# Attention scores in pairs of pairs, a split first eviction and a held value load, in a talking-heads and two-FFN kernel

## The chip, the cores and the metric

The kernel runs on one core of a Trainium2 chip. The metric is the device time of one execution in microseconds (us), lower is better. PE is the matrix engine, PEld its weight loads, DVE the vector engine, ACT the scalar engine, POOL and SP the two engines that here only issue DMAs.

## The reference

Two batches, 12 heads, 448 positions, head size 64, all in float32.

```
scores = einsum('bhij,hg->bgij', q @ k.T / 8, w_pre)      # mix over heads
attn   = softmax(scores)                                   # minus max, exp, over sum
attn   = einsum('bhij,hg->bgij', attn, w_post)             # mix over heads again
x      = (attn @ v)  as (896 tokens, 768)
x      = (h * sigmoid(1.702 h)) @ w_out,  h = x @ w_in     # 768 -> 2048 -> 768
x      = (P(h) / Q(h)) @ w_out2,          h = x @ w_in2    # rational activation
```

## The kernel before, in words

**Attention.** Each batch's 448 query rows are cut into chunks of 120, 120, 120 and 88: eight chunks. For one chunk, `scores` (L293) makes the raw scores of six **pairs** of heads. The two heads of a pair have 64 rows of contraction each, so their two matmuls stand in the two halves of the PE array and run side by side; one pair fills one of two PSUM buffers `mm` (two banks, one head in each). `scores_out` (L295, copies at L229 on ACT and L231 on DVE) evicts a pair to the SBUF tile `S`. When all six pairs of a chunk are in `S`, SP issues its `regroup` DMAs (L313), one for each **group** of 10 query rows: they lay 10 rows by 12 heads on 120 partitions (`T`). A group then goes through `pre` (L318, the first head mix on PE), `rowmax` on DVE (L324), `expo` on ACT (L330), three small steps on DVE or ACT (L336 to L344) that put 1/sum into the second mixing matrix `W`, `post` (L351, the second head mix, four matmuls) and `post_out` (L229, to `AT`). There are 90 groups. After a chunk's last group, `av` (L370) multiplies by `v`, 24 matmuls for each half of the heads.

**The two FFNs.** They begin in the last groups' shadow (L576 to L578 up, L643 to L645 down). Their weights are loaded by POOL's queue and worked on by ACT and DVE during attention and after it.

**Order.** Nothing is ordered by a run-time scheduler. `Plan.issue` (L103) lays out all steps ahead of time: each step has an engine (or several to choose from), an assumed length, the steps it depends on, the buffers that it takes and gives back, and a rank; a free engine gets the ready step of lowest rank whose buffers are free. The result is one fixed order for each engine; on the chip, semaphores make an instruction wait for its inputs. Where PE would be idle for long in the plan, `fill` (L221, L223) puts in matmuls on a tile of ones (`warm`).

**Start.** SP issues six loads of `k` (one for each pair, L280), then the mixing matrices, then the second chunk's `q`; ACT issues the first chunk's `q`; POOL issues the four loads of the first batch's `v` (L285), with nothing to wait for on the chip. The first chunk's pairs are evicted by ACT or DVE, one engine a pair, as the plan chooses (`sco0`).

Of the kernel before, what the change touches and what calls it, by code (L numbers as in the profile page):

```python
# [20 lines left out]
CP = 112  # L21
NJ = S // CP
NP = H // 2
# [43 lines left out]
class Plan:  # L67
# [9 lines left out]
        self.fill = fill  # L77
        self.fill_from = fill_from

    def add(self, name, ways, deps, rank, emit=None, take=(), give=(), lag=0):  # L80

        assert name not in self.steps
        self.steps[name] = (list(ways), list(deps), rank, emit, take, give, lag)

    def taker(self, n, b):

# [16 lines left out]
    def issue(self):  # L103
        steps, slots = self.steps, self.slots
        succ = {n: [] for n in steps}
        left, at, on = {}, dict.fromkeys(steps, 0), {}
        for n, s in steps.items():
            left[n] = len(s[1])
            for d in s[1]:
                succ[d].append(n)  # L110
        idle = dict.fromkeys(("sp", "pe", "act", "dve", "pool"), 0)
        ready = {e: [] for e in idle}
        dry = set()
        events = [(0, 1, n) for n in steps if not left[n]]
        heapq.heapify(events)
        order = []

        runs, more = [], sum(s[0][:1] != [] and s[0][0][0] == "pe" for s in steps.values())

        def busy(now):  # L120
            return sum(min(z, now) - max(a, now - FILL_WIN) for a, z in runs if z > now - FILL_WIN)

        def done(n, now):
            for b in steps[n][5]:
                b, h = b if isinstance(b, tuple) else (b, self.taker(n, b))
                slots[b][slots[b].index(h)] = None
                dry.clear()
            for m in succ[n]:
                who = [w[0] for w in steps[m][0]]
                hop = HOP.get((on.get(n), who == [on.get(n)]), 0) + 80 * (who == ["pe"]) if who else 0  # L130
                at[m] = max(at[m], now + hop)
                left[m] -= 1
                if not left[m]:
                    heapq.heappush(events, (at[m], 1, m))

        while events and events[0][0] < 1e8:
            now = events[0][0]
            while events and events[0][0] == now:
                _, kind, n = heapq.heappop(events)
                if kind == 0 or (kind == 1 and not steps[n][0]):  # L140
                    done(n, now)
                elif kind == 1:
                    for e, ns, wait in steps[n][0]:
                        if wait:
                            heapq.heappush(events, (now + wait, 3, (n, e, ns)))
                        else:
                            insort(ready[e], (steps[n][2], n, ns))
                            dry.discard(e)
                elif kind == 3 and n[0] not in on:
                    insort(ready[n[1]], (steps[n[0]][2], n[0], n[2]))  # L150
                    dry.discard(n[1])
            for e in idle:
                if idle[e] > now:
                    continue
                for _, n, ns in () if e in dry else ready[e]:
                    take, lag = steps[n][4], steps[n][6]
                    if n not in on and all(self.pick(b) is not None for b in take):
                        for b in take:
                            k = self.bank[n, b] = self.pick(b)
                            slots[b][k] = n  # L160
                            self.uses[b] = k + 1
                        ready[e] = [x for x in ready[e] if x[1] not in on and x[1] != n]
                        idle[e] = now + ns
                        on[n] = e
                        heapq.heappush(events, (now + ns + lag, 0, n))
                        heapq.heappush(events, (now + ns, 2, n))
                        order.append(n)
                        if e == "pe":
# [34 lines left out]
def talking_heads_then_two_ffn(ctx: ExitStack, tc: tile.TileContext, q, k, v, wpre, wpost, win1, wout1, win2, wout2, ab, out):  # L203
# [73 lines left out]
    def load_k(b, hp):  # L277
        if hp == 0:
            t_["k", b] = ap1.tile([128, NP, S], F32, tag="k", name=f"k{b}")
        sp.dma_start(t_["k", b][:, hp], k[b, :, hp])  # L280

    def load_v(b, jc):
        if jc == 0:
            t_["v", b] = ap1.tile([CP, NJ, H * D], F32, tag="v", name=f"v{b}")
        (sp if b else pool).dma_start(t_["v", b][:, jc], v[b, :, jc])  # L285

# [5 lines left out]
            r = slice(o * 64, o * 64 + 64)  # L292
            pe.matmul(p[:M, o, :S], t_["q", ci][r, hp, :M], t_["k", b][r, hp], start=True, stop=True)  # L293

    def scores_out(ci, hp, eng):  # L295
        M = CHUNKS[chunks[ci][1]][1]
        if hp == 0:
            if two_s(ci):

                if ci < NC:  # L300
                    x = f(keep.tile([128, 2, KK, S], F32R, tag="x1", name=f"S{ci}")).rearrange("p a k s -> p (a k) s")
                else:
                    x = f(keep.tile([128, H * S], F32R, tag="wu", name=f"S{ci}")).rearrange("p (h s) -> p h s", h=H)
                t_["S", ci] = x[:IC]
            else:
                t_["S", ci] = ap1.tile([IC, H, S], F32, tag="S", name=f"S{ci}")
        cast(eng, t_["S", ci][:M, 2 * hp : 2 * hp + 2], t_["sc", ci, hp][:M, :, :S])

    def regroup(t):
        ci, gi, n, _ = groups[t]  # L310
# [113 lines left out]
        plan.add(name, (), deps, 0, give=give)  # L424

    step(("mixld",), "sp", 900, [], RANK["k"] + 0.5, load_mix, lag=DMA_LAG)
    step(("mix",), "dve", 200, [("mixld",)], -2, scale_mix)
    for b in range(B):
        f0 = first[b * NC]
        for hp in range(NP):  # L430
            step(("kld", b, hp), "sp", 640 if b else 800, [("scdone", b * NC - 1)] if b else [], f0 + RANK["k"] + 0.01 * hp, load_k, b, hp, take=[] if hp else ["k"], lag=DMA_LAG)
        for jc in range(NJ):
            d0 = [("av", b * NC - 1, 1)] if b else [("rg", 5)]
            step(("vld", b, jc), "sp" if b else "pool", 640, d0, f0 + RANK["v"] + RANK["step_v"] * jc, load_v, b, jc, take=[] if jc else ["v"], lag=DMA_LAG)
    for ci, (b, c) in enumerate(chunks):
        M = CHUNKS[c][1]
        f0, l0 = first[ci], last[ci]
# [1 line left out]
        d0 = [("kld", 0, NP - 1)] if ci == 1 else [("qld", ci - 1)] if ci else []  # L439
        step(("qld", ci), "sp" if ci else "act", 683, d0, f0 + RANK["q"] - 20 * (ci == 1), load_q, ci, take=["q"], lag=DMA_LAG)  # L440
        for hp in range(NP):
            step(("sc", ci, hp), "pe", 800, [("qld", ci), ("kld", b, hp)], f0 + RANK["sc"] + 0.1 * hp, scores, ci, hp, take=["mm"])
            d0 = [("sco", ci, 0)] if hp else []
            step(("sco", ci, hp), copying(2 * S, "sco" if ci > 1 else "sco0", True), 0, [("sc", ci, hp)] + d0, f0 + RANK["sco"] + 0.1 * hp, scores_out, ci, hp, None, take=[] if hp else ["S2" if two_s(ci) else "S"], give=["mm"])
        mark(("scdone", ci), [("sc", ci, hp) for hp in range(NP)], [("q", ("qld", ci))] + ([("k", ("kld", b, 0))] if end_b else []))
        for t in range(f0, l0 + 1):
            step(("rg", t), "sp", 1200, [("sco", ci, hp) for hp in range(NP)], t + RANK["rg"], regroup, t, take=["T"], lag=RG_LAG if ci else 2500)
# [10 lines left out]
        mark(("rgdone", ci), [("rg", t) for t in range(f0, l0 + 1)], [("S2" if two_s(ci) else "S", ("sco", ci, 0))])  # L458
        for a in range(2):
            d0 = [("av", ci, 0)] if a else [("phi", t) for t in range(f0, l0 + 1)] + [("vld", b, jc) for jc in range(NJ)]  # L460
            fin = [("AT", ("phi", f0))] + ([("v", ("vld", b, 0))] if end_b else []) if a else []
# [405 lines left out]
```

## Time and profile before

| what | value |
|---|---|
| runs shown | 728.86, 726.19, 727.99 us; median 727.99 us |
| profiled execution, own time | 726.84 us |
| its span, first to last instruction | 725.1 us |
| PE busy | 712.6 us (98% of the span) |
| DVE / ACT / POOL busy | 559.4 / 408.2 / 159.2 us |

The profiled execution's time is 1.74 us more than its span, which lies before the first and after the last instruction, and 1.15 us under the median. The rows come from that execution; times in them count from the start of the span. Matmuls overlap in the rows (one starts before the one ahead has ended), so what PE spends on a piece of work is read from the start of one row to the start of the next.

### The profile page before, as it was taken

Reading aid. Unit: us, or ns where it says so; the run is one execution under the profiler, and the core shown is the slowest. Engines: PE = TensorE matmul, PEld = TensorE weight load, DVE = VectorE, ACT = ScalarE, POOL = GpSimd, SP = SyncE. Lnnn points to the kernel's source line nnn. Section 1 sums busy time; section 2 is a strip of 40 time slices with the busy share of each in tenths; the row PEclk is TensorE's granted clock in tenths of the full one; section 3 lists DMA queues with packets and bytes.
Section 4 is the critical chain, followed back from the end, with each engine's and each line's share of the span. In section 5 each row is a group of like instructions: output and inputs, shape, how many; then the busy total and the mean of one; then the engine's idle time right before and its main releaser. Section 6 shows DMA issues by size and latency. Waiting matters only on the chain.

```text
span 725.1 us, 11626 instructions
## 1 busy us (share of the span) xinstructions
PE 712.6 (98%) x4224; PEld 599.7 (83%) x4224; DVE 559.4 (77%) x1108; ACT 408.2 (56%) x762; POOL 159.2 (22%) x296
## 2 busy tenths in 40 slices
PE   7999999999999999999999999999999999999997
PEld 4567657666677889999999999999999999999996
DVE  0577877677988579888988888978999589879732
ACT  3686676776677455455443444338887565356310
POOL 1023422222322243433432333210001101000000
PEclk9999999999999999999999999999999999999999
DMA  6667877497646364555545454322102211200122
GB/s 199 228 187 257 255 277 254 150 281 250 231 135 206 122 221 145 200 167 181 192 144 185 153 174 153 133 80 73 44 24 72 88 37 58 66 30 19 39 80 103
DMA packets 39368, 106.86 MB, mean 147 GB/s; under 512 B 6478, under 2 KB 19022, under 8 KB 39310
## 3 DMA queue, kind: packets, MB, share of 16 engines
q0 software_dynamic: 22848, 76.89, 32.4%
q1 hardware_dynamic: 16318, 28.85, 12.0%
q8 instruction: 33, 0.54, 0.3%
q10 hardware_dynamic: 144, 0.37, 0.1%
q14 instruction: 25, 0.20, 0.1%
HBM read 71.49 MB, written 15.34 MB: 120 GB/s over the span
## 4 chain that ended last, share of the span: by engine, by line
PE 66%; DMA 2%; DVE 1%; ACT 1%; issue 0%; ACTq 0%; DVEq 0%; SPq 0%
PE mm L643 11%; PE mm L645 11%; PE mm L644 11%; PE bk L577 11%; PE bk L578 11%; PE bk L576 10%; DMA d1d<-wmk 1%; PE bk L351 1%; DMA d1u<-wm 1%; PE bk L370 1%; PE bk L318 0%; DMA cab<-in_ab_dram 0%; ACT L586 0%; DVE wu L234 0%; ACT wmk L535 0%
## 5 line engine op out<-in xcount | busy, mean ns | idle before, releaser
L643 PE MATMUL mm<-g,wd 128*128 128x448 f32 x384 | 141.9, 370 | 0.0
L645 PE MATMUL mm<-g,wd 128*128 128x448 f32 x384 | 140.5, 366 | 0.0
L644 PE MATMUL mm<-g,wd 128*128 128x448 f32 x384 | 140.4, 366 | 0.0
L351 PEld LDWEIGHTS bk<-W,E 120*112 120x112 f32 (+1 forms) x720 | 84.1, 177 | 36.6 <-issue 22.7
L351 PE MATMUL bk<-W,E 120*112 120x120 f32 (+1 forms) x720 | 89.2, 269 | 1.0 <-ACT E L330 0.8
L318 PE MATMUL bk<-T,wpr 120*120 120x448 f32 (+1 forms) x180 | 82.8, 552 | 1.0 <-DVE xh L234 0.5
L530 POOL DMA_DIRECT2D rawk<-in_win_dram x81 | 44.3, 554 | 163.5 <-ACT rawk L523 34.5
L643 PEld LDWEIGHTS mm<-g,wd 128*128 128x128 f32 x384 | 72.2, 188 | 5.8
L645 PEld LDWEIGHTS mm<-g,wd 128*128 128x128 f32 x384 | 72.2, 188 | 5.7
L644 PEld LDWEIGHTS mm<-g,wd 128*128 128x128 f32 x384 | 72.3, 188 | 5.3
L324 DVE TENSOR_REDUCE sm<-bk 120x1 f32<-120x448 f32 (+1 forms) x90 | 55.8, 620 | 26.2 <-PE bk L318 25.7
L576 PE MATMUL bk<-xh,wu 128*128 128x448 f32 x192 | 70.7, 368 | 1.5 <-ACT t L586 1.5
L577 PE MATMUL bk<-xh,wu 128*128 128x448 f32 x192 | 70.3, 366 | 0.5 <-DVE wu L234 0.5
L577 PE MATMUL bk<-xn,wu 128*128 128x448 f32 x192 | 70.4, 367 | 0.0
L576 PE MATMUL bk<-xn,wu 128*128 128x448 f32 x192 | 70.4, 367 | 0.0
L578 PE MATMUL bk<-xn,wu 128*128 128x448 f32 x192 | 70.4, 367 | 0.0
L578 PE MATMUL bk<-xh,wu 128*128 128x448 f32 x192 | 70.2, 366 | 0.0
L237 DVE TENSOR_TENSOR yt<-mm,yt 128x896 f32<-128x896 f32 (+1 forms) x43 | 40.2, 936 | 37.0 <-PE mm L645 36.8
L229 ACT ACTIVATE AT<-bk 112x480 f32<-112x480 f32 (+1 forms) x87 | 50.4, 579 | 30.7 <-PE bk L351 30.0
L530 POOL DMA_DIRECT2D rawk<-in_wout_dram x70 | 38.5, 555 | 103.2 <-ACT W L342 18.7
L330 ACT ACTIVATE E<-bk,sm 120x448 f32<-120x448 f32 (+1 forms) x90 | 56.3, 627 | 2.6 <-DVE sm L338 1.2
L597 DVE SCALAR_TENSOR_TENSOR t<-t,cab,bk 128x448 f32<-128x448 f32 x64 | 43.4, 678 | 15.8 <-ACT t L593 10.8
(102 smaller groups left out, 1303.3 us busy)
## 6 DMA issues: line engine op xcount, KB each, us to landing
rawk<-in_win_dram POOLq DMA_DIRECT2D x81, 256.0 KB, 4.0
T<-S SPq DMA_DIRECT2D x86, 210.0 KB
rawk<-in_wout_dram POOLq DMA_DIRECT2D x70, 256.0 KB, 3.4
raw<-in_wout_dram POOLq DMA_DIRECT2D x26, 256.0 KB, 3.4
d1d<-wmk POOLq DMA_DIRECT2D x22, 256.0 KB, 4.4
d1u<-wmk POOLq DMA_DIRECT2D x28, 192.0 KB, 4.9
rawk<-d1u POOLq DMA_DIRECT2D x14, 384.0 KB, 3.3
raw<-in_win_dram POOLq DMA_DIRECT2D x15, 256.0 KB, 3.7
```

The lines of the kernel that those rows point to most:

```text
L229: act.activation(o, i, AF.Copy)
L318: pe.matmul(p[:K, :S], wpr[:K, :K], t_["T", t][:K], start=True, stop=True)
L324: dve.tensor_reduce(t_["sm", t][:K, 0:1], t_["pre", t][:K, :S], AX.X, ALU.max, negate=True)
L330: act.activation(t_["E", t][:K], t_["pre", t][:K, :S], AF.Exp, bias=sm[:K, 0:1], scale=1.0, accum_out=sm[:K, 1:2])
L351: pe.matmul(o, t_["E", t][:K, jc * CP : jc * CP + CP], t_["W", t][:K], start=True, stop=True)
L530: pool.dma_start(r[:, c : c + 256], src[:, c : c + 256])
L576: pe.matmul(p[:, :S], w[:, 0, ws], x[:, 0, kk], start=kk == 0, stop=False)
L577: pe.matmul(p[:, :S], w[:, 1, ws], x[:, 0, kk], start=False, stop=False)
L578: pe.matmul(p[:, :S], w[:, 0, ws], x[:, 1, kk], start=False, stop=kk == KK - 1)
L643: pe.matmul(p[:, hf, :S], w[:, 0, ms], gt[:, 0, i, cs], start=i == 0, stop=False)
L644: pe.matmul(p[:, hf, :S], w[:, 1, ms], gt[:, 0, i, cs], start=False, stop=False)
L645: pe.matmul(p[:, hf, :S], w[:, 0, ms], gt[:, 1, i, cs], start=False, stop=i == FQ - 1)
```

## The change

Three things. First, POOL's first `v` load now waits: a new step `vhold` on ACT copies four numbers of the second group's exponents into the tile `v`, and the load that overwrites them has to come after. Second, each pair of the first chunk is evicted by both engines, one head by ACT and the other by DVE. Third, from the second chunk on, a pair with an even number may only be placed when both `mm` buffers are free (`need=2`), and the odd pair behind it has the rank -99, so that it follows at once: the scores come in visits of two pairs. The plan lays out all steps anew with these rules, so the order changes on PE, ACT, DVE and, little, on SP; POOL's order stays, but for the wait. The two FFNs' part of the order stays.

```diff
-    def add(self, name, ways, deps, rank, emit=None, take=(), give=(), lag=0):
+    def add(self, name, ways, deps, rank, emit=None, take=(), give=(), lag=0, need=1):
...
-                    if n not in on and all(self.pick(b) is not None for b in take):
+                    if n not in on and all(self.pick(b) is not None and slots[b].count(None) >= need for b in take):
...
+    def hold_v():
+
+        t_["v", 0] = ap1.tile([CP, NJ, H * D], F32, tag="v", name="v0")
+        act.activation(t_["v", 0][:1, :, 0], t_["E", 1][:1, :NJ], AF.Copy)
...
-        cast(eng, t_["S", ci][:M, 2 * hp : 2 * hp + 2], t_["sc", ci, hp][:M, :, :S])
+        hs = slice(0, 2) if o is None else slice(o, o + 1)
+        cast(eng, t_["S", ci][:M, 2 * hp : 2 * hp + 2][:, hs], t_["sc", ci, hp][:M, hs, :S])
...
+    step(("vhold",), "act", 200, [("exp", 1)], -40, hold_v, take=["v"])
...
-            d0 = [("av", b * NC - 1, 1)] if b else [("rg", 5)]
+            d0 = [("av", b * NC - 1, 1)] if b else [("vhold",)]
...
-            step(("sc", ci, hp), "pe", 800, [("qld", ci), ("kld", b, hp)], f0 + RANK["sc"] + 0.1 * hp, scores, ci, hp, take=["mm"])
+
+            two = ci > 0
+            d0 = [("qld", ci), ("kld", b, hp | two)] + ([("sc", ci, hp - 1)] if two and hp % 2 else [])
+            rk = -99 if two and hp % 2 else f0 + RANK["sc"] + 0.1 * hp
+            step(("sc", ci, hp), "pe", 800, d0, rk, scores, ci, hp, take=["mm"], need=2 if two and hp % 2 == 0 else 1)
...
+            if ci == 0:
+
+                step(("sco", ci, hp), "act", 430, [("sc", ci, hp)] + d0, rk, scores_out, ci, hp, None, 0, take=[] if hp else [S_])
+                step(("sco1", ci, hp), "dve", 520, [("sc", ci, hp), ("sco", ci, 0)], rk, scores_out, ci, hp, None, 1)
+                mark(("scend", hp), [("sco", ci, hp), ("sco1", ci, hp)], [("mm", ("sc", ci, hp))])
```

Three places of the order follow. In the rows, a matmul that writes `mm` from `k,q` is one pair of scores (x2, its two heads), one with `wpr` is a group's `pre`, one that reads `W,E` (x4) is a group's `post`, one that reads `AT,v` (x24) is `av`.

PE, the third chunk's scores, in the kernel before (behind the last row shown, the second `av` stands at "..."):

```order
L293 MATMUL mm_64<-k_82,q_310 120x448 x2
L293 MATMUL mm_65<-k_82,q_310 120x448 x2
L351 MATMUL bk_66<-W_363,E_339 112x120 x4
L293 MATMUL mm_64<-k_82,q_310 120x448 x2
L318 MATMUL bk_67<-T_281,wpr 120x448
L293 MATMUL mm_65<-k_82,q_310 120x448 x2
L351 MATMUL bk_68<-W_380,E_357 112x120 x4
L293 MATMUL mm_64<-k_82,q_310 120x448 x2
L318 MATMUL bk_69<-T_294,wpr 120x448
L351 MATMUL bk_66<-W_396,E_376 112x120 x4
L370 MATMUL bk_67<-AT_223,v_201 64x120 x24
...
L293 MATMUL mm_65<-k_82,q_310 120x448 x2
```

The same place in the changed kernel:

```order
L298 MATMUL mm_64<-k_82,q_312 120x448 x2
L298 MATMUL mm_65<-k_82,q_312 120x448 x2
L357 MATMUL bk_67<-W_375,E_350 112x120 x4
L324 MATMUL bk_68<-T_281,wpr 120x448
L357 MATMUL bk_69<-W_391,E_369 112x120 x4
L324 MATMUL bk_66<-T_296,wpr 120x448
L298 MATMUL mm_64<-k_82,q_312 120x448 x2
L298 MATMUL mm_65<-k_82,q_312 120x448 x2
L376 MATMUL bk_67<-AT_230,v_204 64x120 x24
L376 MATMUL bk_68<-AT_230,v_204 64x120 x24
L298 MATMUL mm_64<-k_82,q_312 120x448 x2
L298 MATMUL mm_65<-k_82,q_312 120x448 x2
```

Five visits have become three. Counted over the whole order between the first `post` and the first FFN matmul, 27 visits become 18; there are 36 pairs in both. Neighbours of a score and a head-mix matmul (`pre` or `post`) go from 48 to 29, of a score and an `av` from 6 to 7, of an `av` and a head mix from 8 to 7.

PE from the second chunk's first pair to the first `post`, in the kernel before:

```order
L293 MATMUL mm_64<-k_82,q_119 120x448 x2
L293 MATMUL mm_65<-k_82,q_119 120x448 x2
L293 MATMUL mm_64<-k_82,q_119 120x448 x2
L318 MATMUL bk_66<-T_133,wpr 120x448
L293 MATMUL mm_65<-k_82,q_119 120x448 x2
L318 MATMUL bk_67<-T_143,wpr 120x448
L293 MATMUL mm_64<-k_82,q_119 120x448 x2
L293 MATMUL mm_65<-k_82,q_119 120x448 x2
L318 MATMUL bk_68<-T_149,wpr 120x448
L318 MATMUL bk_69<-T_154,wpr 120x448
L318 MATMUL bk_66<-T_160,wpr 120x448
L351 MATMUL bk_67<-W_190,E_172 112x120 x4
```

And in the changed kernel:

```order
L298 MATMUL mm_64<-k_82,q_122 120x448 x2
L298 MATMUL mm_65<-k_82,q_122 120x448 x2
L324 MATMUL bk_66<-T_135,wpr 120x448
L298 MATMUL mm_64<-k_82,q_122 120x448 x2
L298 MATMUL mm_65<-k_82,q_122 120x448 x2
L324 MATMUL bk_67<-T_149,wpr 120x448
L324 MATMUL bk_68<-T_155,wpr 120x448
L298 MATMUL mm_64<-k_82,q_122 120x448 x2
L298 MATMUL mm_65<-k_82,q_122 120x448 x2
L324 MATMUL bk_69<-T_160,wpr 120x448
L324 MATMUL bk_66<-T_165,wpr 120x448
L357 MATMUL bk_67<-W_202,E_175 112x120 x4
```

Three pairs stood ahead of the first `pre`, and two do now; six pairs and five `pre` stand ahead of the first `post` in both. Ahead of these rows stand 10 fill matmuls before and 12 now.

DVE at the start, with the semaphores that each row waits for, in the kernel before (the copies into `S_111` evict the first chunk):

```order
L242 MEMSET warm 128x240
L231 COPY S_111<-mm_64 120x896 [waits PE_49,Activation_49]
L253 TENSOR_SCALAR wpr<-wsrc 120x120 [waits DMAHW7_49]
L231 COPY S_147<-mm_64 120x896 [waits PE_49,Activation_49]
L324 TENSOR_REDUCE sm_162<-bk_66 120x1 [waits PE_49]
```

And in the changed kernel:

```order
L242 MEMSET warm 128x240
L231 COPY S_111<-mm_64 120x448 [waits Activation_49]
L231 COPY S_111<-mm_65 120x448 [waits Activation_49]
L231 COPY S_111<-mm_64 120x448 [waits Activation_49]
L231 COPY S_111<-mm_65 120x448 [waits Activation_49]
L253 TENSOR_SCALAR wpr<-wsrc 120x120 [waits DMAHW7_49]
L231 COPY S_111<-mm_64 120x448 [waits Activation_49]
L231 COPY S_111<-mm_65 120x448 [waits Activation_49]
L330 TENSOR_REDUCE sm_167<-bk_66 120x1 [waits PE_49]
```

DVE evicted one whole pair of the first chunk, and now half of each of the six. Each half waits on ACT's semaphore, for ACT's half of the same pair (the first for a count of 1, the second for 2, and so on), and not on PE's.

## Rows read from the trace of the kernel before

**Rows 1.** The page: busy time, then the granted TensorE clock in 40 slices.
```profile
PE 712.6 (98%) x4224; PEld 599.7 (83%) x4224; DVE 559.4 (77%) x1108; ACT 408.2 (56%) x762; POOL 159.2 (22%) x296
...
PEclk9999999999999999999999999999999999999999
```

**Rows 2.** Busy time of each engine, clock, DMA share, GB/s in two stretches.
```profile
2.00:14.40 12.40, 9.61 (x30) 5.00 (x31) 1.31 (x2) 2.30 (x4) 1.51 (x3) 1.00 0.96 287
28.17:239.40 211.23, 209.28 (x1684) 145.30 (x1682) 165.58 (x458) 153.68 (x343) 54.47 (x100) 1.00 0.68 223
```

**Rows 3.** DMA issues of the first 32 us, KB of each.
```profile
k<-in_k_dram SPq DMA_DIRECT2D x6, 224.0 KB
v<-in_v_dram POOLq DMA_DIRECT2D x4, 336.0 KB, 7.8
...
q<-in_q_dram ACTq DMA_DIRECT2D x1, 360.0 KB
```

**Rows 4.** Timeline of the start: start, length, engine, line, count, idle before.
```profile
1.18 3.34 PE L223 MATMUL bk<-warm 128*128 128x240 f32 x14 [1.18 <-DVE warm L242]
...
1.28 2.23 POOL L285 DMA_DIRECT2D v<-in_v_dram  x4 [0.83 <-POOLq L854]
...
5.18 3.35 PE L293 MATMUL mm<-k,q 64*120 64x448 f32 x8 [0.66 <-DMA q<-in_q_dram]
...
9.55 1.85 PE L293 MATMUL mm<-k,q 64*120 64x448 f32 x4 [1.01 <-ACT S L229]
...
12.51 4.56 PE L293 MATMUL mm<-k,q 64*120 64x448 f32 x12 [1.11 <-DMA k<-in_k_dram]
...
17.00 1.38 PE L223 MATMUL bk<-warm 128*128 128x240 f32 x10
17.11 0.92 ACT L229 ACTIVATE S<-mm 120x896 f32<-120x896 f32 x1 [0.30 <-PE mm L293]
18.05 13.37 SPq L313 DMA_DIRECT2D T<-S  x16
...
21.29 1.01 PE L318 MATMUL bk<-T,wpr 120*120 120x448 f32 x2
...
28.17 1.80 PE L351 MATMUL bk<-W,E 120*112 120x120 f32 x16
```

**Rows 5.** Timeline of PE, in the third chunk's scores and in plain groups.
```profile
43.25 1.77 PE L293 MATMUL mm<-k,q 64*120 64x448 f32 x8
44.95 1.07 PE L351 MATMUL bk<-W,E 120*112 120x120 f32 x8
45.95 1.02 PE L293 MATMUL mm<-k,q 64*120 64x448 f32 x4
46.90 1.01 PE L318 MATMUL bk<-T,wpr 120*120 120x448 f32 x2
47.84 1.02 PE L293 MATMUL mm<-k,q 64*120 64x448 f32 x4
...
60.19 0.92 PE L318 MATMUL bk<-T,wpr 120*120 120x448 f32 x2
60.94 0.98 PE L351 MATMUL bk<-W,E 120*112 120x120 f32 x8
61.76 0.92 PE L318 MATMUL bk<-T,wpr 120*120 120x448 f32 x2
```

**Rows 6.** Groups of instructions by line and shape: busy us, mean ns, idle before.
```profile
L324 DVE TENSOR_REDUCE sm<-bk 120x1 f32<-120x448 f32 x86 | 53.3, 620 | 25.3 <-PE bk L318 24.8
...
L229 ACT ACTIVATE AT<-bk 112x480 f32<-112x480 f32 x83 | 48.1, 580 | 27.9 <-PE bk L351 27.3
...
L229 ACT ACTIVATE S<-mm 120x896 f32<-120x896 f32 x29 | 26.4, 916 | 18.7 <-PE mm L293 18.7
```

**Rows 7.** The longest PE wait between 28.2 and 239.4; then PE after attention (timeline).
```profile
PE bk L351 <- ACT E L330: 0.8, 1, 0.8
...
254.94 0.48 PE L576 MATMUL bk<-xh,wu 128*128 128x448 f32 x1 [1.49 <-ACT t L586]
```

More of the change, by code (lines that the diff above doesn't have):

```diff
@@ L78, in __init__ @@
         self.fill_from = fill_from
-    def add(self, name, ways, deps, rank, emit=None, take=(), give=(), lag=0):
+    def add(self, name, ways, deps, rank, emit=None, take=(), give=(), lag=0, need=1):
         assert name not in self.steps
-        self.steps[name] = (list(ways), list(deps), rank, emit, take, give, lag)
+        self.steps[name] = (list(ways), list(deps), rank, emit, take, give, lag, need)
     def taker(self, n, b):
@@ L155, in issue @@
                 for _, n, ns in () if e in dry else ready[e]:
-                    take, lag = steps[n][4], steps[n][6]
-                    if n not in on and all(self.pick(b) is not None for b in take):
+                    take, lag, need = steps[n][4], *steps[n][6:]
+                    if n not in on and all(self.pick(b) is not None and slots[b].count(None) >= need for b in take):
                         for b in take:
@@ L280, in load_k @@
         sp.dma_start(t_["k", b][:, hp], k[b, :, hp])
+    def hold_v():
+        t_["v", 0] = ap1.tile([CP, NJ, H * D], F32, tag="v", name="v0")
+        act.activation(t_["v", 0][:1, :, 0], t_["E", 1][:1, :NJ], AF.Copy)
     def load_v(b, jc):
-        if jc == 0:
+        if b and jc == 0:
             t_["v", b] = ap1.tile([CP, NJ, H * D], F32, tag="v", name=f"v{b}")
@@ L293, in scores, with scores_out @@
             pe.matmul(p[:M, o, :S], t_["q", ci][r, hp, :M], t_["k", b][r, hp], start=True, stop=True)
-    def scores_out(ci, hp, eng):
+    def scores_out(ci, hp, eng, o=None):
         M = CHUNKS[chunks[ci][1]][1]
-        if hp == 0:
+        if hp == 0 and not o:
             if two_s(ci):
@@ L432, in talking_heads_then_two_ffn @@
         for jc in range(NJ):
-            d0 = [("av", b * NC - 1, 1)] if b else [("rg", 5)]
-            step(("vld", b, jc), "sp" if b else "pool", 640, d0, f0 + RANK["v"] + RANK["step_v"] * jc, load_v, b, jc, take=[] if jc else ["v"], lag=DMA_LAG)
+            d0 = [("av", b * NC - 1, 1)] if b else [("vhold",)]
+            step(("vld", b, jc), "sp" if b else "pool", 640, d0, f0 + RANK["v"] + RANK["step_v"] * jc, load_v, b, jc, take=["v"] if b and not jc else [], lag=DMA_LAG)
     for ci, (b, c) in enumerate(chunks):
@@ L441, in talking_heads_then_two_ffn @@
         for hp in range(NP):
-            step(("sc", ci, hp), "pe", 800, [("qld", ci), ("kld", b, hp)], f0 + RANK["sc"] + 0.1 * hp, scores, ci, hp, take=["mm"])
-            d0 = [("sco", ci, 0)] if hp else []
-            step(("sco", ci, hp), copying(2 * S, "sco" if ci > 1 else "sco0", True), 0, [("sc", ci, hp)] + d0, f0 + RANK["sco"] + 0.1 * hp, scores_out, ci, hp, None, take=[] if hp else ["S2" if two_s(ci) else "S"], give=["mm"])
+            two = ci > 0
+            d0 = [("qld", ci), ("kld", b, hp | two)] + ([("sc", ci, hp - 1)] if two and hp % 2 else [])
+            rk = -99 if two and hp % 2 else f0 + RANK["sc"] + 0.1 * hp
+            step(("sc", ci, hp), "pe", 800, d0, rk, scores, ci, hp, take=["mm"], need=2 if two and hp % 2 == 0 else 1)
+            S_ = "S2" if two_s(ci) else "S"
+            d0 = [("sco", ci, 0)] if hp else []
+            rk = f0 + RANK["sco"] + 0.1 * hp
+            if ci == 0:
+                step(("sco", ci, hp), "act", 430, [("sc", ci, hp)] + d0, rk, scores_out, ci, hp, None, 0, take=[] if hp else [S_])
+                step(("sco1", ci, hp), "dve", 520, [("sc", ci, hp), ("sco", ci, 0)], rk, scores_out, ci, hp, None, 1)
+                mark(("scend", hp), [("sco", ci, hp), ("sco1", ci, hp)], [("mm", ("sc", ci, hp))])
+            else:
+                ways = copying(2 * S, "sco" if ci > 1 else "sco0", True)
+                step(("sco", ci, hp), ways, 0, [("sc", ci, hp)] + d0, rk, scores_out, ci, hp, None, take=[] if hp else [S_], give=["mm"])
         mark(("scdone", ci), [("sc", ci, hp) for hp in range(NP)], [("q", ("qld", ci))] + ([("k", ("kld", b, 0))] if end_b else []))
         for t in range(f0, l0 + 1):
-            step(("rg", t), "sp", 1200, [("sco", ci, hp) for hp in range(NP)], t + RANK["rg"], regroup, t, take=["T"], lag=RG_LAG if ci else 2500)
+            step(("rg", t), "sp", 1200, [("sco", ci, hp) for hp in range(NP)] + [("sco1", ci, hp) for hp in range(NP) if not ci], t + RANK["rg"], regroup, t, take=["T"], lag=RG_LAG if ci else 2500)
             step(("pre", t), "pe", 770, [("rg", t)] + ([] if t else [("mix",)]), t + RANK["pre"], pre, t, take=["bk"], give=[("T", ("rg", t))])
@@ L460, in talking_heads_then_two_ffn @@
             d0 = [("av", ci, 0)] if a else [("phi", t) for t in range(f0, l0 + 1)] + [("vld", b, jc) for jc in range(NJ)]
-            fin = [("AT", ("phi", f0))] + ([("v", ("vld", b, 0))] if end_b else []) if a else []
+            fin = [("AT", ("phi", f0))] + ([("v", ("vld", b, 0) if b else ("vhold",))] if end_b else []) if a else []
             step(("av", ci, a), "pe", 2600 * M // IC, d0, l0 + RANK["av"], av, ci, a, take=["bk"], give=fin)
```

## Prediction

> **What bounds the kernel now.** I read the page first. PE is busy for 712.6 of 725.1 us [rows 1], so time can only come from what PE does, or from its few gaps. The windows divide the span: a start up to the first `post` at 28.17, attention from there to the first FFN matmul at 239.40 (211.23 us, PE busy for 209.28), and the FFNs [rows 2]. The change touches the first two. They have different limits, which the timelines show.
>
> At the start PE isn't the limit. Between 2.0 and 14.4 us the DMA engines are 0.96 busy and move 287 GB/s [rows 2], about 3.56 MB. In that stretch fall the first `q` (360 KB), six `k` (1,344 KB), four `v` (1,344 KB) [rows 3], the mixing matrices and the second `q`. The scores wait for it: the fourth pair starts at 12.51 after 1.11 us of waiting for a DMA of `k` [rows 4]. The last eviction ends at 18.03, SP issues the first regroup at 18.05, and the first `pre` runs at 21.29 [rows 4].
>
> The start is also slow because PE is at the lower of its two clock levels (1.2 GHz), although the page's clock row shows full speed everywhere [rows 1]: 14 fill matmuls take 3.34 us at 1.18, 0.24 each, and 10 take 1.38 at 17.00, 0.14 each [rows 4]. Two pairs take 3.35 us at 5.18. The clock rose late in the gapless run that begins at 12.51; neither the 3.34 nor the 3.35 us before had raised it.
>
> In attention PE is the limit. A plain group costs 60.19 to 60.94 to 61.76, that is 0.75 for `pre` and 0.82 for `post` [rows 5], and waits are rare: the longest is 0.8 [rows 7].
>
> **Price of a visit.** Two pairs together cost 43.25 to 44.95, 1.70; one pair alone costs 45.95 to 46.90, 0.95 [rows 5]. The second pair of a visit thus costs 0.75 and the edges of a visit cost 0.20. The neighbours pay too: the `post` between two visits takes 1.00 (44.95 to 45.95) where a plain one takes 0.82, and the `pre` 0.94 (46.90 to 47.84) where a plain one takes 0.75 [rows 5]: 0.09 an edge. One edge between scores and a head mix costs 0.10 + 0.095 = 0.195.
>
> The order has 48 such edges before and 29 after, between the first `post` and the FFN. 19 x 0.195 = **3.7 us less**. Edges with `av` go from 8 and 6 to 7 and 7; I cost that at nothing, since only the kind of neighbour changes.
>
> **The start without `v`.** What the first chunk's scores need is 1,704 KB, 1.74 MB; at the 287 GB/s of the stretch that is 6.1 us instead of the ten that pass until 12.5. With the first bytes at about 2 us the last `k` is in at about 8.1. Then PE never waits for `k`, and the pairs go:
> - Pairs 0 to 2 at the low clock, 1.55 each (3.35 less a tail of 0.25, halved): starts at 5.2, 6.8 and 8.5.
> - The clock rose inside the gapless run of 4.56 from 12.51, since the fills right behind it are at the high level. As an estimate I let it rise as far into the run that now begins at 5.2, near 9.6. Pair 2 ends at 9.9.
> - From then on evictions set the pace. The copy of 896 columns takes ACT 0.916, one of 480 takes 0.580: 0.55 for a half. DVE reads 448 columns in 0.620 [rows 6]. The order says that DVE's half waits for ACT's half of the same pair, so the halves lie behind each other: 0.55 + 0.62 and about 0.15 of handing over, 1.3, longer than ACT's 0.92 alone. A `mm` buffer goes round in 1.0 (a pair that PE waited for, at the high clock) + 1.4, and there are two: 1.2 a pair. Pairs 3, 4 and 5 end at 11.0, 12.3 and 13.4; with the last eviction SP issues at 14.7.
>
> That is 18.05 - 14.7 = 3.3 us earlier, and the first `pre` at about 18.0 instead of 21.29. The split itself gives nothing: with ACT alone the same reckoning ends at 14.0.
>
> The order gives some of it back: between the first `pre` and the first `post` stood .94, .95, .94, 1.70 and three `pre` (28.17 - 21.29 = 6.88 [rows 4]). Now it is .94, 1.70, 2 x .85, 1.70, .85 + .75 = 7.64, because a pair that ran while PE waited for `T` now runs behind. 3.3 - 0.76 = **2.5 us less**.
>
> Bounds of this term: if the clock stays low for all six pairs, they end at 14.8, SP issues at 16.1 (1.9 earlier, 1.1 net); if the fills and the first visit are slow too (12 x 0.24 + 3.35 = 6.2), the first `pre` is at 21.0 and the term is -0.5. If the clock rises at the third pair, the term is 3.0.
>
> The Trainium skill ("TensorE: Matmul & The Clock Gate", part 1) says that the moment of the rise differs from run to run of one kernel; no run shown here can tell, and by it any value between these bounds could turn up in a single execution.
>
> **What else moves.** The hold costs ACT one copy of four numbers, under 0.3, behind the second group's exponents at about 23; `v` is then issued at 24 and, by its 7.8 us to landing [rows 3], is in at 32 to 35 beside the regroup DMAs. `av` wants it near 49. Nothing else stands behind it on POOL until the weights, which wait for group 8. If that cover failed, every us after 49 would count.
>
> New waits: the halves of the scores' evictions come in lumps of two (1.8 us of ACT's or DVE's time), beside a group's own work on ACT, so exponents and `post_out` come later in some places; before the first `post`, an eviction of the second chunk stands on DVE ahead of a rowmax. The 211.23 us hold some 3 us of waits and small losses already (the sum of the prices above gives 208.0). I take **0.6 us more**, between 0 and 4.
>
> The FFNs keep their order. PE's wait at 254.94 is for ACT's activation [rows 7], which itself follows the end of attention, so it moves along.
>
> **Sum.** 3.7 + 2.5 - 0.6 = 5.6 us, 726.84 - 5.6 = 721.2 for an execution like the profiled one. The median of the runs shown is 1.15 above it; I forecast the median, 727.99 - 5.6 = **722.4 us**. A difference under 0.5% (3.6 us) is about what a measurement of this kernel can't tell from no change.
>
> **The rivals.**
> 1. *The start gains little* (the clock stays low, or falls in the wait of about 1.3 us that PE now has ahead of the first `pre`). For it: the gaps of 1.0 and 1.1 us at 9.55 and 12.51 lay in a stretch that stayed low [rows 4]. Against: the wait of 1.49 at 254.94 is followed by a matmul of 0.48, as at 2.4 GHz [rows 7]. Net 0.5 instead of 2.5: **724.4**. The Trainium skill ("TensorE: Matmul & The Clock Gate", part on HAM oscillation) warns that idle stretches of PE bring the low clock back; the trace of the kernel before has no such fall up to the FFN.
> 2. *Two-pair visits make PE wait.* For it: ACT is busy 153.68 of 211.23 us and DVE 165.58 [rows 2], and a visit adds 1.8 us of evictions in a lump. Against: the visit at 43.25 was of two pairs and no wait followed [rows 5]. At 0.15 us a visit, 18 visits take 2.7 more: **725.1**.
> 3. *The FFNs take it back*: weights are late for an attention that ends earlier, and the time is **728**. Against: PE's waits there are short, DMA traffic is low, and the late buffers open when attention ends.
> 4. *Slower.* Each visit now demands both buffers, and evictions lag far enough that PE stands for 0.5 us or more at each of the 18: 9 us of waits against 6.2 of gains, **731**. It decides from 0.34 a visit (no gain) and 0.55 (slower by 0.5%). No wait in [rows 5] speaks for it.
> 5. *The change doesn't do what it says*: the split is no split in time, since the order makes it serial; that is in the sum already. The Trainium skill ("PSUM — Partial Sum Buffer", section on bank collisions) says that two engines may read different banks at once, and the halves are in different banks; by it alone the start would be 0.6 better, 721.8, but the program's wait forbids it.
>
> **How the numbers follow.** Forecast 0.56 (own range 720.4 to 724.3), rival 1 0.16, rival 2 0.14, rival 3 0.07, rival 4 0.05, more than forecast (below 720) 0.02. Rivals 1 and 2 lie on both sides of the 0.5% bound at 724.35: about half of 1 and a third of 2 are faster by over 0.5%, and about 0.54 of the forecast is. So 0.69 faster, 0.26 within 0.5%, 0.05 slower. The range for 8 in 10 reaches from 719.8 to 726.4: it takes in rivals 1 and 2 and the start's bounds, and leaves out 3 and 4.
>
> **What would show it.** In the profile after: the first `v` issue at about 24 us; no wait for `k`; SP's first regroup near 14.7 and the first `pre` near 18.0; DVE's copies of 448 columns each beginning after ACT's end; the first `post` near 25.7; visits of 1.70 and only those; 211.2 shrunk to about 208 between the first `post` and the FFN. Wrong would make it: fills and pairs at 0.24 and 1.5 us behind the first chunk, waits of PE for ACT or DVE behind the visits, or an FFN stretch longer than 483.6.

## The result, and the profile after

| | median (range), runs | before, same chip | ratio, 95% interval |
|---|---|---|---|
| changed kernel | 719.08 us (717.47 to 720.82), 4 | 727.09 us | 0.9888 [0.9864, 0.9913] |
| changed kernel, run again | 717.93 us (715.65 to 720.23), 6 | 726.82 us | 0.9875 [0.9853, 0.9897] |

The change is worth 8.0 us, and 8.9 in the second session. 5.6 were forecast, and 719.08 lies under the lower end of the range, 719.8: the sign was right, and the sum was too small.

The page of the profiled execution (719.9 us, span 718.1), beside [rows 1]:

```profile
PE 706.3 (98%) x4226; PEld 599.1 (83%) x4226; DVE 558.2 (78%) x1111; ACT 407.8 (57%) x766; POOL 160.4 (22%) x296
```

PE lost 6.3 us of busy time and the span 7.0. The windows cut as in [rows 2], first `post` to first FFN matmul and from there on:

```profile
24.94:232.14 207.20, 204.79 (x1683) 145.82 (x1682) 161.82 (x456) 154.82 (x345) 56.24 (x102) 1.00 0.72 233
232.14:716.00 483.86, 479.62 (x2463) 442.62 (x2461) 387.07 (x638) 243.29 (x404) 102.57 (x188) 1.00 0.34 112
```

The first `post` comes 3.23 us earlier (28.17 to 24.94), the attention stretch is 4.03 shorter (211.23 to 207.20), and from the first FFN matmul to the end it is 0.26 longer (485.70 to 485.96, from the spans): 7.0 in all.

The third chunk's first visits, to be read beside [rows 5]:

```profile
40.82 1.77 PE L298 MATMUL mm<-k,q 64*120 64x448 f32 x8 [0.62 <-DMA q<-in_q_dram]
42.51 1.07 PE L357 MATMUL bk<-W,E 120*112 120x120 f32 x8
43.42 0.92 PE L324 MATMUL bk<-T,wpr 120*120 120x448 f32 x2
```

From start to start a visit of two pairs takes 1.69 here and the `post` behind it 0.91 (one edge), as priced.

The start, to be read beside [rows 4]:

```profile
5.14 5.67 PE L298 MATMUL mm<-k,q 64*120 64x448 f32 x16 [0.63 <-DMA q<-in_q_dram]
...
7.04 0.55 ACT L229 ACTIVATE S<-mm 120x448 f32<-120x448 f32 x1 [4.58 <-PE mm L298]
...
7.62 0.62 DVE L231 COPY S<-mm 120x448 f32<-120x448 f32 x1 [6.50 <-ACT S L229]
...
13.18 0.55 ACT L229 ACTIVATE S<-mm 120x448 f32<-120x448 f32 x1 [0.54 <-PE mm L298]
13.75 0.62 DVE L231 COPY S<-mm 120x448 f32<-120x448 f32 x1 [0.46 <-ACT S L229]
14.41 14.13 SPq L319 DMA_DIRECT2D T<-S  x16
...
17.30 1.01 PE L324 MATMUL bk<-T,wpr 120*120 120x448 f32 x2 [0.94 <-DMA T<-S]
...
23.54 2.23 POOL L290 DMA_DIRECT2D v<-in_v_dram  x4 [23.09 <-ACT v L285]
...
24.94 1.80 PE L357 MATMUL bk<-W,E 120*112 120x120 f32 x16
```

Four pairs run without a gap from 5.14, and no wait for `k` is left. Each DVE half begins when ACT's half of its pair has ended: the split eviction is serial, as the order said. SP's first regroup is at 14.41 (14.7 forecast), the first `pre` at 17.30 (18.0), the first `post` at 24.94 (25.7), and POOL's first `v` at 23.54 (24).

PE's waits in the attention stretch, beside [rows 7] (what PE waited for: total us, times, longest):

```profile
PE bk L324 <- ACT AT L229: 1.8, 1, 1.8
PE mm L298 <- DMA q<-in_q_dram: 0.6, 1, 0.6
```

In the kernel before PE waited 2.0 us in all in this stretch, 0.8 at most [rows 7]; now it waits 2.4. The 0.6 is for the third chunk's `q`. The 1.8 ends at 156 us, and ACT's timeline there shows

```profile
152.24 0.20 ACT L336 ACTIVATION_READ_ACCUMULATOR E<-bk,sm 120x1 f32 x1
154.74 0.89 ACT L555 ACTIVATE wmk<-rawk 128x768 f32<-128x768 f32 x1 [2.30 <-DMA d1d<-wmk]
155.53 0.56 ACT L229 ACTIVATE AT<-bk 112x480 f32<-112x480 f32 x1
```

ACT stands 2.30 us at a step of the FFN weights until a store of weights to DRAM (`d1d`) has landed. The `post_out` behind it is late, and PE stands for the PSUM buffer that it would give back. No eviction of a visit is in this chain, and the wait isn't new in kind. ACT stood at the same step in the kernel before, twice (the first two rows); the third row is the changed kernel's second time:

```profile
160.74 0.90 ACT L535 ACTIVATE wmk<-rawk 128x768 f32<-128x768 f32 x1 [1.56 <-DMA d1d<-wmk]
227.73 0.94 ACT L535 ACTIVATE wmk<-rawk 128x768 f32<-128x768 f32 x1 [2.34 <-DMA d1d<-wmk]
219.38 0.92 ACT L555 ACTIVATE wmk<-rawk 128x768 f32<-128x768 f32 x1 [0.51 <-DMA d1d<-wmk]
```

Behind the first of these PE waited 0.8 us for exponents, at 162 us. Behind the second it waited 0.2 and 0.5 for DVE's evictions of `av` (`xh`), at 231 and 232, where DVE was working on those weights in between. Behind the third it doesn't wait. So the new order moved ACT's waits for stores about: one grew and one shrank.

### The profile page after: what moved, and what is told of

Its sections match the earlier page's. It is cut to its first block, busy times and chain, and to the rows that moved or that the text cites. A ratio compares the mean times of both kernels' runs of the same rounds, so it can differ in the third digit from the quotient of the medians.

```text
span 718.1 us, 11630 instructions
## 1 busy us (share of the span) xinstructions
PE 706.3 (98%) x4226; PEld 599.1 (83%) x4226; DVE 558.2 (78%) x1111; ACT 407.8 (57%) x766; POOL 160.4 (22%) x296
## 4 chain that ended last, share of the span: by engine, by line
PE 92%; DMA 5%; ACT 1%; DVE 0%; issue 0%; POOL 0%; ACTq 0%; SPq 0%
PE mm L663 11%; PE mm L665 11%; PE mm L664 11%; PE bk L597 10%; PE bk L596 10%; PE bk L598 10%; PE bk L357 9%; PE bk L324 9%; PE bk L376 5%; PE mm L298 5%; DMA q<-in_q_dram 2%; DMA d1d<-wmk 1%; DMA raw<-in_wout_dram 1%; DMA T<-S 0%; DVE S L231 0%
```

## The experiments

Theory A is the prediction's mechanism part by part, sized by the traces of both kernels. The texts on record name its rivals. "Stretch" is the time from the first `post` to the first FFN matmul in a profiled execution. Twelve runs follow, each beside the kernel before on the same chip.

### One part at a time

**The hold alone** (on the kernel before):

```diff
+    step(("vhold",), "act", 200, [("exp", 1)], -40, hold_v, take=["v"])
...
-            d0 = [("av", b * NC - 1, 1)] if b else [("rg", 5)]
+            d0 = [("av", b * NC - 1, 1)] if b else [("vhold",)]
```

> The kernel before with the held value load alone (no split, no two-pair visits). Theory A (three separate terms: the hold brings the first pre-mix forward by some 4 us, the visits save 19 edges x 0.195 = 3.7 us, the split costs a little): first pre-mix near 17.3 us, the order behind it as before, so the whole 4.0 us stay: 723.1 against 727.1 of before. Theory B (the split pays: two engines on the first evictions are what brings the start forward): first pre-mix not before 19, 725 or more. Theory C (luck of the order: a new plan moves PE's waits about, and the parts don't add up): any time within 2.5 us of A's.

Measured: 722.61 us against 726.94, ratio 0.9946 [0.9928, 0.9964]. Timeline of the start, and the stretch:

```profile
14.26 5.83 SPq L319 DMA_DIRECT2D T<-S  x7
...
17.43 1.01 PE L324 MATMUL bk<-T,wpr 120*120 120x448 f32 x2
```

```profile
24.31:236.22 211.91, 209.32 (x1683) 145.23 (x1682) 165.52 (x458) 153.88 (x343) 55.99 (x103) 1.00 0.70 229
...
PE mm L298 <- DMA q<-in_q_dram: 1.6, 1, 1.6
```

The first `post` is 3.9 us earlier and the median 4.3. The stretch keeps its busy time (209.32, 209.28 in [rows 2]). Without the visits the order from `pre` to `post` stays as before, so the 0.76 isn't given back here. The last row is a wait of PE at 39 us for the third chunk's `q`. Three profiles with the hold have such a wait (1.6 here, 0.6 in the changed kernel, 1.5 in the last run but one below), others with the hold haven't, and none without it. `v` is now under way when this `q` is issued; that it delays the `q` is likely, but not shown.

**The split alone** (on the kernel before):

```diff
+                step(("sco", ci, hp), "act", 430, [("sc", ci, hp)] + d0, rk, scores_out, ci, hp, None, 0, take=[] if hp else [S_])
+                step(("sco1", ci, hp), "dve", 520, [("sc", ci, hp), ("sco", ci, 0)], rk, scores_out, ci, hp, None, 1)
```

> The kernel before with the split first evictions alone. Theory A: the scores still wait for k, the last pair is evicted in 0.55 + 0.62 us one behind the other instead of 0.92, the first regroup is issued 0.3 us later: 727.4. Theory B: the start gains 1 us or more: 726 or less. Theory C: within 2.5 us of 727.4, by waits later in attention.

Measured: 727.21 against 726.94, 1.0003 [0.9984, 1.0022]. SP's first regroup is at 17.92 (18.05 before). While `k` is late, the way of evicting has no worth.

**The visits alone** (on the kernel before):

```diff
-            step(("sc", ci, hp), "pe", 800, [("qld", ci), ("kld", b, hp)], f0 + RANK["sc"] + 0.1 * hp, scores, ci, hp, take=["mm"])
...
+            step(("sc", ci, hp), "pe", 800, d0, rk, scores, ci, hp, take=["mm"], need=2 if two and hp % 2 == 0 else 1)
```

> The kernel before with the visits of two pairs alone. Its order has 30 edges between scores and head mixes instead of 48: 18 x 0.195 = 3.5 us less; with two pairs instead of three ahead of the first pre-mix, 0.8 more. Theory A: 727.1 - 3.5 + 0.8 = 724.4, no wait of PE behind a visit. Rival (two-pair visits make PE wait for evictions): 726 or more. Theory C: within 2.5 us of 724.4.

Measured: 721.86 against 726.94, 0.9941 [0.9924, 0.9958]: 5.1 us, where the edges alone (18 fewer here, 3.5) less the order's 0.7 give 2.8. So the visits bring some 2 us more than their edges. Its profiled execution took 727.01, the slowest of eleven (the others 720.54 to 722.40), and shows why. PE waited 2.4 us at one place (again for a `post_out` behind a store of weights), and the windows behind it read:

```profile
157.00:160.30 3.30, 1.25 (x10) 0.86 (x8) 0.84 (x3) 1.05 (x2) 0.00 (x0) 1.00 0.64 247
160.30:167.10 6.80, 6.44 (x17) 3.00 (x18) 4.99 (x13) 3.52 (x9) 1.28 (x3) 0.50 0.52 192
```

Behind the wait the granted clock is 0.50 of 2.4 GHz for 6.8 us; 6.44 busy us at half speed hold 3.2 us of work.

**All but the split** (the changed kernel, first chunk's pairs evicted whole):

```diff
-            if ci == 0:
...
-                step(("sco1", ci, hp), "dve", 520, [("sc", ci, hp), ("sco", ci, 0)], rk, scores_out, ci, hp, None, 1)
...
-            else:
```

> The changed kernel without the split: hold and visits, the first chunk's pairs evicted whole, one engine a pair. Theory A: first regroup issued at about 13.9 instead of 14.4 us, 718.5 against 719.1 of the changed kernel. Theory B: the first regroup is issued later than 14.4, 721 or more. Theory C: within 2.5 us of 718.5.

Measured: 718.01 against 726.94, 0.9885 [0.9864, 0.9906]; the first regroup is at 14.07, 0.34 earlier than with the split.

```profile
24.67:231.11 206.44, 204.72 (x1683) 145.82 (x1682) 161.88 (x456) 154.56 (x345) 56.56 (x102) 1.00 0.72 234
...
PE bk L324 <- ACT AT L229: 1.7, 1, 1.7
```

Beside the hold alone only the visits differ. The medians differ by 4.6 (722.61 to 718.01), the order's 0.7 included (pre to post 6.88 there, 7.61 here), so the stretch is worth 5.3. The edges are 3.7 of it. The other 1.6 are rough, since the interval of each ratio is some 1.3 to 1.5 us to either side. In the two profiled executions the stretch lost 5.5 (211.91 to 206.44): PE's busy time 4.6, its idle time 0.9. The hold alone had the wait of 1.6 for `q`, which this execution hasn't; instead it has the one of 1.7 behind the store.

### What moves from run to run

**The changed kernel again**, unchanged:

```diff
 (no edit)
```

> The changed kernel again, unaltered, beside the others on the same chip, because four runs of it spread over 3.4 us. If its median of 719.1 was the typical time: 718.5 to 719.7. If those four runs lay low by chance and the profiled execution (719.9) is typical: 719.7 to 720.8.

Measured: 717.93 (715.65 to 720.23). The profiled execution is its slowest, 720.23; around 156 us its windows are

```profile
150.00:156.40 6.40, 3.95 (x25) 2.83 (x24) 3.66 (x11) 3.03 (x7) 0.00 (x0) 1.00 0.72 262
156.40:159.80 3.40, 3.40 (x10) 1.14 (x8) 2.67 (x9) 1.76 (x6) 0.00 (x0) 0.50 0.66 238
160.00:165.00 5.00, 5.00 (x30) 2.94 (x28) 3.71 (x9) 4.00 (x11) 2.66 (x5) 1.00 0.68 225
```

ACT waits 2.96 us for the same store (2.30 in the first profile), PE 2.4 instead of 1.8, and now the clock falls to 0.50 for 3.4 us. The longer wait (0.7) and the low clock (half of 3.4) are 2.4 us, and this execution lies 2.3 above the median. The five others, whose clock stayed up, still spread from 715.65 to 718.65.

**One-pair visits** (the changed kernel; both `mm` buffers are still demanded, but no pair follows at once):

```diff
-            d0 = [("qld", ci), ("kld", b, hp | two)] + ([("sc", ci, hp - 1)] if two and hp % 2 else [])
-            rk = -99 if two and hp % 2 else f0 + RANK["sc"] + 0.1 * hp
+            d0 = [("qld", ci), ("kld", b, hp | two)]
+            rk = f0 + RANK["sc"] + 0.1 * hp
...
-            step(("sc", ci, hp), "pe", 800, d0, rk, scores, ci, hp, take=["mm"], need=2 if two and hp % 2 == 0 else 1)
+            step(("sc", ci, hp), "pe", 800, d0, rk, scores, ci, hp, take=["mm"], need=2 if two else 1)
```

> The changed kernel with visits of one pair throughout: 38 visits and 67 edges between scores and head mixes instead of 18 and 29 (edges with av 14 in both). If an edge costs 0.195 us: 38 x 0.195 = 7.4 us more, 726.5, and the stretch from the first post-mix to the first FFN matmul goes from 207.2 to about 214.6. If most of the gain in attention was rarer waits and not edges: 722 or less.

Measured: 728.70 against 726.82, 1.0026 [1.0007, 1.0045], and 10.8 above the changed kernel. The order has 67 edges instead of 29; 38 x 0.195 = 7.4. The rest is waits (the profile is of the slowest of the twelve executions, 734.25: PE's waits, then one window):

```profile
PE bk L324 <- DMA T<-S: 4.3, 3, 1.7
PE bk L324 <- ACT E L336: 2.0, 2, 1.4
PE bk L324 <- ACT AT L229: 1.8, 2, 0.9
```

```profile
231.00:237.80 6.80, 6.46 (x50) 5.19 (x52) 3.79 (x10) 1.06 (x4) 0.27 (x1) 0.50 0.22 80
```

The direction is the edges'; the size doesn't isolate their price, since waits come with it.

**A later plan for the weights** (the changed kernel; the plan reckons 6,000 ns instead of 4,500 until a weight store has landed, so that what follows it is placed later):

```diff
-            step(("est", key), "pool", 2000 * c, [("wb", key, 3)], e, w_store, key, give=[("wm", ("wmag", key))], lag=W_LAG)
+            step(("est", key), "pool", 2000 * c, [("wb", key, 3)], e, w_store, key, give=[("wm", ("wmag", key))], lag=6000)
```

> The changed kernel with one number of the plan altered: it now reckons 6,000 instead of 4,500 ns for a weight tile's store to land, so that ACT's next weight step on that buffer stands later in ACT's order. 30 edges instead of 29 (0.2 us). If PE's wait of 0.8 to 2.6 us near 152 us comes from ACT standing at that step until the store has landed: the wait is gone, 716.7 with runs within 2 us of each other (717.9 with 4.6 us of spread before). If the DMA traffic there delays PE in another way too (regroups, k): the wait comes back under another name, 717.5 or more.

Measured: 732.01 against 727.0, 1.0067 [1.0045, 1.009]: a miss by 15. The wait at 156 is gone (the longest PE wait in attention is 0.2), but the FFN's weights are late:

```profile
PE bk L596 <- ACT wu L229: 2.8, 1, 2.8
PE bk L596 <- ACT xh L229: 2.7, 1, 2.7
```

```profile
231.88:722.60 490.72, 484.90 (x2502) 448.60 (x2501) 392.33 (x641) 247.24 (x410) 105.02 (x194) 0.99 0.34 111
...
263.95 9.57 PE L223 MATMUL bk<-warm 128*128 128x240 f32 x84
```

From the first FFN matmul to the end it is 14 us more (231.88 to 731.8, 499.9 against 485.96), and that is the whole loss. PE waits twice, and the clock is at 0.50 behind both (248.3 to 251.7 and 275.6 to 282.4). Most of it is the last row: the plan saw PE without weights at 264 us and put in 84 fill matmuls, 9.57 us, where the changed kernel has 14 in 1.73; then comes the wait of 2.8. The order of the weights also changed with the number, so this isn't the wait's removal alone. It is the loss of the prediction's rival 3, brought about by a number of the plan: the FFN has little slack.

### The start

**Halves side by side** (the changed kernel; each head of the first chunk in a one-bank PSUM tile of its own):

```diff
-            step(("sc", ci, hp), "pe", 800, d0, rk, scores, ci, hp, take=["mm"], need=2 if two and hp % 2 == 0 else 1)
...
+                step(("sc0", hp), "pe", 400, d0, rk, score_head, hp, 0, take=["bk"], need=2)
+                step(("sc", ci, hp), "pe", 400, [("sc0", hp)], -99, score_head, hp, 1, take=["bk"])
```

> The changed kernel, with the two heads of each first-chunk pair in two separate one-bank PSUM tiles instead of one two-bank tile; in the order DVE's halves then wait for PE and no longer for ACT. If the serial halves cost what the trace says (0.55 + 0.62 us behind each other): halves overlap, pairs come at 0.9 to 1.0 us instead of 1.1 to 1.25, the first regroup is issued near 13.3 us instead of 14.4, 718.0. If ACT and DVE can't read PSUM side by side at full speed: halves of 0.8 us or more, 719 or more, no gain.

Measured: 716.80 against 726.82, 0.9861 [0.984, 0.9882].

```profile
5.14 7.00 PE L303 MATMUL bk<-k,q 64*120 64x448 f32 x24 [0.62 <-DMA q<-in_q_dram]
...
7.02 0.54 ACT L229 ACTIVATE S<-bk 120x448 f32<-120x448 f32 x1 [4.55 <-PE bk L303]
7.06 0.62 DVE L231 COPY S<-bk 120x448 f32<-120x448 f32 x1 [5.94 <-PE bk L303]
...
12.88 1.76 SPq L326 DMA_DIRECT2D T<-S  x2
```

```profile
23.49:228.86 205.37, 204.73 (x1684) 145.84 (x1682) 161.87 (x456) 154.52 (x345) 55.96 (x102) 1.00 0.72 235
```

ACT and DVE now read their banks at the same time, and SP's regroup is 1.53 us earlier than in the changed kernel. So two engines can read two banks at once; the changed kernel's halves were serial because they shared a tile. The stretch is the shortest of all, and PE's one wait in it is 0.6, again at the store.

**Three more fills** ahead of the first pair, on the halves side by side:

```diff
+        more = [3]
...
-            for _ in range(2):
+            for _ in range(2 + (more.pop() if more else 0)):
```

> e5_parallel with three more fill matmuls ahead of the first pair, so that PE doesn't stand from 4.5 to 5.1 us. If unbroken PE work from 1.2 us on raises the clock earlier: first three pairs partly at 2.4 GHz, but then k sets the pace (estimate from the changed kernel's windows: last k near 8), so the first regroup at 11.5 to 12.5 us, 717. If the clock doesn't rise earlier for it: as e5_parallel, within 0.3 us.

Measured: 715.19 against 726.82, 0.9837 [0.9817, 0.9858]: the best kernel here, 2.7 under the changed one in the same session.

```profile
1.18 3.98 PE L225 MATMUL bk<-warm 128*128 128x240 f32 x17 [1.18 <-DVE warm L244]
...
5.38 5.26 PE L305 MATMUL bk<-k,q 64*120 64x448 f32 x24 [0.22 <-DMA q<-in_q_dram]
...
11.38 9.08 SPq L328 DMA_DIRECT2D T<-S  x11
```

The gap ahead of the first pair shrinks from 0.63 us to 0.22, and all six pairs run in 5.26, where they took 7.00 without the fills: the clock was up from the first pair on (in the granted clock at 5.4; 9.1 without the fills).

**The same fills on the kernel before**, same diff:

> The kernel before with three more fill matmuls ahead of the first pair, v as before. If the fills raise the clock near 5.4 us as they did in e9_bridge: the pairs then wait for k alone (pair 3 at 12.5, the last at about 14.3, evicted by 16.2), first pre-mix near 19.4 instead of 21.3, 725.0 against 726.9. That would split the start's gain into the clock's share (1.9) and the rest, which needs v out of the way. If the clock doesn't rise, or k is later than that: 726.5 or more.

Measured: 726.84 against 727.0, 0.9998 [0.9986, 1.0009].

```profile
5.42 2.02 PE L295 MATMUL mm<-k,q 64*120 64x448 f32 x8 [0.37 <-DMA q<-in_q_dram]
...
10.10 1.02 PE L295 MATMUL mm<-k,q 64*120 64x448 f32 x4 [2.66 <-DMA k<-in_k_dram]
...
13.32 4.84 PE L295 MATMUL mm<-k,q 64*120 64x448 f32 x12 [2.21 <-DMA k<-in_k_dram]
```

The two first pairs are fast (2.02 instead of 3.35), but the third starts at 10.10 all the same: PE waits longer for `k`, and the clock falls again from 11.6 to 18.4. With `v` in the way, the earlier rise is worth nothing here.

**Whole pairs, ACT and DVE in turn**, with the hold, the visits and the fills:

```diff
             if ci == 0:
+                ways = [w for w in ways if w[0] == ("act", "dve")[hp % 2]]
```

> Hold and visits, three more fills, the first chunk's pairs evicted whole, ACT and DVE in turn. ACT takes 0.92 and DVE 1.09 us a pair side by side, about 1.05 us a pair at the high clock; first regroup near 12 us, and the order has four pairs instead of two ahead of the first pre-mix (first pre-mix to first post-mix 5.8 instead of 7.6 us, but PE reaches the first pre-mix only when those four are done, near 15.5). First post-mix at about 21.5: 715. If the fixed work behind the pre-mixes sets the first post-mix instead: 22.5 or later, 716 or more.

Measured: 717.88 against 727.0, 0.9877 [0.9857, 0.9897]. The start came as expected (first regroup 12.38, first `post` 21.75), but the stretch is 208.34, with two waits, at 37 and 153 us:

```profile
PE mm L300 <- DMA q<-in_q_dram: 1.5, 1, 1.5
PE bk L326 <- ACT AT L231: 1.4, 1, 1.4
```

In the profiles the start gains 3.2 us over the changed kernel (24.94 to 21.75) and the stretch gives 1.1 back; the medians are the same (717.88 here, 717.93 there in another session). The rest of the difference isn't explained.

**The halves side by side, the fills and the later plan** together (the diffs of those three):

> All that helped together: the changed kernel with separate PSUM tiles for the first chunk's halves, three more fills, and the 6,000 ns for weight stores. If the three add up: e9_bridge (715.2) less the wait of 1.7 us at 150 us plus one edge: 713.7. If the wait returns elsewhere: 715 or more.

Measured: 729.18 against 727.0, 1.0041 [1.0027, 1.0055]. It misses for the same reason: the two FFN waits of 2.8 and 2.7 us and the 84 fills are here too.

## Why the prediction was too small

**Right, by mechanism.** The hold frees `k` and is most of the start. The split is serial and gives nothing; it costs 0.34 at the regroup (14.07 without it; from the first pair to the regroup 9.3 us in both profiles of the changed kernel, 8.9 in the hold alone and in all but the split). The clock rose at 9.16 and 9.65 in these two profiles, where 9.6 was assumed. The order from `pre` to `post` gives back 0.76 (17.30 to 24.94 is 7.64, as worked out). A visit is 1.70 in the profile after too. `v` is in time for `av`, and nothing waits for it; what it may cost the third chunk's `q` was not foreseen.

**The failed step: "I take 0.6 us more, between 0 and 4".** The prediction expected new waits behind the visits' lumps of evictions, and bounded them by nothing from below, so the range had no room for fewer. With two-pair visits no profile has a wait of PE for an eviction of scores in the stretch; its waits over 0.3 us there are behind ACT's stores of weights, or for `q`. In the two profiled executions the stretch lost 4.0 where the edges give 3.7: 0.3 less of waits in place of 0.6 more. The medians give, for the visits beyond their edges, 5.3 - 3.7 = 1.6 us less (with the hold), and 5.1 + 0.7 - 3.5 = 2.3 less (without it). So this term was off by 0.9 in the profiles and by 2.2 to 2.9 in the medians; with a bound at minus 2 the range's lower end would have lain 2 us lower and held the time.

Where the waits went can be said in part. Reckoned block by block from starts to starts, at the prices of [rows 5] and with `av` as measured, the stretch comes to 206.8 us before and 203.3 in the changed kernel (an estimate). The edges are thus 3.5, and 4.4 us of waits and small losses stood in the kernel before, not the 3 of the prediction; 3.9 are left in the changed kernel, 3.1 in all but the split, 2.1 in the halves side by side. Two places can be named in the kernel before: the waits behind ACT's two stores, for exponents [rows 7] and for `xh`. The hold alone has both too; the second reads there

```profile
PE bk L324 <- DVE xh L234: 0.5, 1, 0.5
```

and no profile with two-pair visits has such a row. Besides a wait of 0.5 at 98 us in the kernel before, the rest are starts of PE late by less than 0.2 us each, 1.8 us in the kernel before and 1.3 in the changed one. Why these shrank isn't settled; that longer visits leave fewer hand-overs is argued, not shown. Nor is it shown how much of the 1.6 to 2.3 is the order and how much the moment at which stores and `q` happened to land: PE's wait at 156 alone was between 0.6 and 2.4 us in the seven profiles that have it.

**The start, 2.5 forecast, 3.23 measured.** Of the 0.73, 0.29 is the regroup (14.41 for 14.7). The rest is the way from the regroup to the first `pre`, 2.89 us: I took the 3.24 of [rows 4] (18.05 to 21.29), but there PE was still busy with a third pair, while it now waits for `T`.

**The base.** I forecast a median 1.15 above the profiled execution, from three runs. With more runs the kernel before has medians of 726.94, 726.82 and 727.0 (22, 17 and 20 runs), its profiled 726.84. The 1.15 were chance, and made the forecast one more us too high; without that the range's lower end would have been 718.8 and held the time, too. Of the 3.3 us between 722.4 and 719.08, 1.3 are in the profiled executions (721.2 and 719.9: the start 0.7, the stretch 0.9, the FFNs -0.3), 1.15 are the base, and 0.8 is that the changed kernel's profiled execution lies above its median.

**The rivals.**
- 1, the clock at the start: didn't come, with PE's wait of 0.94 ahead of the first `pre`. Its mechanism is real in longer waits, below.
- 2 and 4, visits that make PE wait: refuted: the stretch shrank by more than its edges, and PE's waits for ACT in it (1.8 in the changed kernel, 1.7 in all but the split) are behind a store of weights, not behind evictions of scores.
- 3, the FFN: 0.26 us in the changed kernel, but 14 when the plan was moved.
- 5, the split: serial, as costed. The Trainium skill ("PSUM — Partial Sum Buffer", section on bank collisions) lets two engines read different banks at once. The halves side by side agree: 0.54 and 0.62 us beside each other, and 1.53 us earlier at the regroup.

What stays open: why the weight store lands later in some executions, how much fewer the waits are from one execution to the next, and a plan that avoids the wait at 156 without making the FFN's weights late.

## What to carry to other kernels

When a matrix engine is the limit, count its changes of work in the emitted order and price one edge from starts to starts: 19 edges of 0.195 us were worth about their sum here. Ask of a wait what the engine it names was itself waiting for: behind ACT stood a store. Bound a "new waits" term on both sides, since a new order removes waits as well as it adds them, and take the base from more than three runs. At a start that waits for data, ask first which transfer is in the way of the needed one: neither a faster eviction nor a faster clock gave anything until `v` was moved.

## What the hardware showed that I had not expected

- TensorE's granted clock fell to 0.50 (1.2 GHz) behind single waits of PE of 2.4 us (two kernels), 2.7 and 2.8, for 3.4 or 6.8 us. It didn't behind waits of 1.8 and 1.7 in the changed kernel, nor behind one of 2.7 in the last kernel above. In the split alone it fell at 12.1 us, where PE had waited 1.11 us and was in a second wait of 1.86; in the one-pair visits, behind two waits of 1.6 and 1.7 and in a third of 1.4. So the length of one wait doesn't tell it. In the visits alone such a fall cost 3.2 us on top of the wait.
- In the four profiles with three more fill matmuls the clock was up at 4.5 to 5.4 us, in three of them before the fills had ended; in all the others it rose at 8.7 us or later.
- ACT's wait for a store of weights stands at 151 to 161 us in every profile with the plan's old number, for 0.3 to 3.0 us, though ACT is only 57% busy; what PE loses behind it is from nothing to 2.4 us.
